# Another order in the opening of a fused attention and feed-forward kernel: mask edges, two weight loads, and layer 2 among the value products

## The chip, the cores and the metric

The kernel runs on one core of a Trainium2 chip. The metric is the device time of one execution in microseconds (us), as the median of several runs. Five engines matter: TensorE (PE in the profile; its weight loads are shown apart as PEld), VectorE (DVE), ScalarE (ACT), GpSimd (POOL) and SyncE (SP). They run independently of each other and wait for each other through semaphores. Each engine works through its own instructions in the order in which the program lists them, so an instruction that waits holds back all that stands behind it on its engine.

## The reference

First comes an attention with a window: of 576 positions in each of 8 batches and 8 heads, each attends to those at most 32 away. Its result, 4608 tokens of 512 numbers, goes through a feed-forward block of two matrix products.

```python
scores = scale * np.matmul(q, k.transpose(0, 1, 3, 2))
mask = np.abs(pos[:, None] - pos[None, :]) <= window
scores = np.where(mask, scores, -1000000000.0)
attn = np.exp(scores - max); attn = attn / (sum + 1e-09)
x = np.matmul(attn, v)            # to 4608 x 512
h = x @ w_in                      # 512 x 2048
g = h * (1.0 / (1.0 + np.exp(-1.702 * h)))
out = (g @ w_out).astype(np.float32)   # 2048 x 512
```

Inputs and output are float32 in device memory; the kernel computes in 16-bit types and sums in float32.

## The kernel before, in words

**Units and tiles.** The 4608 tokens are cut into 36 units u of 128 tokens for the attention, and into 9 tiles t of 512 tokens for the feed-forward part; tile t takes units 4t to 4t+3. For one unit the steps are: `scores(u)` (line 248), 24 small products on PE, then two exponentials on ACT, one for each half of the heads, which give `p`; `band(u)` (line 272), one multiplication on DVE of `p` by the mask; `values(u)` (line 280), 16 products on PE, listed as `pv`; `norm(u)` (line 298), a reciprocal and a multiplication on DVE that give `x`. `x_T` or `x_T2` (line 327) then transposes `x` on PE and copies it to `xT` for the first layer.

**Where the results lie.** Products land in the accumulation memory, whose banks have names: "t" (two banks), "A", "B", "C", "E" and, for layer 2, "LA" and "LB". A bank is used again only after its last reader is done: `scores(6, "t")`, `values(4, "t")`, `values(6, "t")` and `x_T2(6, "t", ...)` use "t" in turn, so each waits for the exponential, the norm or the copy that reads the one before. `values(5, "AC")` and `values(7, "AC")` do the same with "A" and "C".

**The mask.** `mask` holds four blocks of 64 columns. Ordinary units use blocks 1 and 3. A unit with a batch border takes block 0 or 2 in their place: `band` (lines 273 to 277) picks block 0 for unit 4, which is the first such unit. `setup_mask` (line 99) writes all four blocks alike; `cut_mask` (line 108), four small fills on POOL (line 111), sets the outer edges of blocks 0 and 2 to zero. Thus `band(4)` must wait for the first two of these fills.

**Values.** `values(u)` reads the rows of `v` as they are (`ve`, from `load_v`, line 194) and shifted by half a unit (`vo`). `odd_v(u)` (line 208) makes `vo` of unit u from two halves, the first of `ve[u+1]` and the second of `ve[u]`, with one copy for each; lines 218 and 220 tell them apart.

**Loads.** All loads are issued by POOL, in the order of the program: `load_kq` (line 125, staging tiles `kst` and `qst`), `load_v` (line 199), `load_v_part` (line 205), `load_w1` (line 115, w_in) and `load_w2(c)` (line 119, quarter c of w_out, 512 KB in the kernel's type). They land in the tiles `w1` and `w2`, both listed as `w`.

**Layers.** In the opening, layer 1 of tile 0 runs as plain products: `layer1_plain` (line 392), eight products of 256 columns into one bank, and a gelu on ACT (line 404). Layer 2 of tile 0 comes from `layer2_plain(0, 0)` and `layer2_plain(0, 1)` (line 478): a list `l2` of 64 single products of 512 columns, here called parts. `do(l2, n)` issues the next n of them. Part 4c' to 4c'+3 read rows 2c' and 2c'+1 of `w2`, so parts 0 to 7 of the list need quarter 0 of w_out, parts 8 to 15 quarter 1, parts 16 to 23 quarter 2 and parts 24 to 31 quarter 3. From tile 1 on both layers multiply with seven products in place of eight; `l1_group` (line 421) is one fourth of layer 1 of a tile, into which parts of layer 2, value products and, for tile 1, transposes of later `k` and `q` (`T_pe`, line 235) are woven. `x_sums` (line 363) makes the sums of `xT` that it needs, and stands between the opening and the first such group.

**The order around the change** is written out by hand in `opening` (line 576) and runs from its first loads to `do(self.l2, 4)` at line 712. After it come `x_sums(1)` and `first_layer1` (line 869), with `fetch` (line 714) issuing the loads of later units.

Of the kernel before, what the change touches and what calls it, by code (L numbers as in the profile page):

```python
# [26 lines left out]
class _Kernel:  # L27
# [548 lines left out]
    def opening(self):  # L576

        nc, dve, act, pool = self.nc, self.nc.vector, self.nc.scalar, self.nc.gpsimd
        self.setup()
        for i in range(8):  # L580
            dve.memset(self.idle[:, 64 * i:64 * i + 64], 0.0)
        dve.memset(self.spark, 0.0)
        for t in self.ve:
            dve.memset(t[:, :, self.D:], 1.0)
        self.load_first("k", 0)
        self.load_first("q", 0)
        make_identity(nc, self.ident)
        act.activation(self.spark, self.spark, AF.Exp)
        for u in (0, 1, 2):
            self.load_v(u)  # L590
        self.load_first("k", 1)
        self.load_first("q", 1)
        self.load_w1(0)
        self.setup_mask()
        self.load_v(3)
        self.load_v_part(512, 64)
        self.load_w1(1)
        self.load_w1(2)
        self.load_four("k")
        self.odd_v(3, pool)  # L600
        self.load_four("q")
        self.load_w1(3)
        self.load_v_part(576, 64)
        dve.tensor_copy(self.identh, self.ident)
        self.keep_busy(30, "E", 192)
        self.T_first("k", 0, "AC", (dve, act))
        self.keep_busy(3, "E", 512)
        self.T_first("q", 0, ("LA", "LB"), (dve, act))
        self.keep_busy(4, "E")
        self.load_v(5)  # L610
        self.load_w2(0)
        self.load_v(6)
        self.load_v(7)
        self.load_v_part(1024, 64)
        self.load_w2(1)
        self.load_v_part(1088, 64)
        for c in (2, 3):
            self.load_w2(c)
        self.load_kq("k", 8)
        self.scores(0, "t")  # L620
        self.scores(1, "AC")
        self.odd_v(0, dve)
        self.odd_v(1, dve, (1,))
        self.keep_busy(6, "E")
        self.band(0)
        self.odd_v(1, dve, (0,))
        self.band(1)
        self.values(0, "t")
        self.keep_busy(4, "E")
        self.values(1, "AC")  # L630
        self.norm(0)
        self.norm(1)
        self.T_first("k", 1, "BE", (act, act))
        self.T_first("q", 1, ("LA", "LB"), (act, dve))
        self.x_T(0, "B", dve)
        self.x_T(1, "E", dve)
        self.odd_v(2, dve, (1,))
        self.scores(2, "t")
        self.scores(3, "AC")
        gelus = []  # L640

        def l1(half, d, tag):
            self.layer1_plain(0, d, half, tag)

        l1(0, 0, "B")
        l1(0, 1, "E")
        self.band(2)
        self.odd_v(2, dve, (0,))
        self.band(3)
        self.values(2, "t")  # L650
        self.norm(2)
        self.values(3, "AC")
        self.norm(3)
        self.keep_busy(4, "LA", 512)
        l1(0, 2, "LA")
        self.x_T2(2, "A", dve)
        l1(0, 3, "LB")
        dve.tensor_copy(self.k_first, self.kT[0][:, :, 0:64])
        dve.tensor_copy(self.v_first, self.ve[0][0:64])
        for i in (3, 1, 2):  # L660
            self.w1_sums((i,), 0)
        self.cut_mask()
        for u in (6, 7):
            self.odd_v(u, pool)
        for u in (8, 9, 10, 11):
            self.fetch(u)
        l1(1, 0, "B")
        l1(1, 1, "E")
        l1(1, 2, "LA")
        l1(1, 3, "LB")  # L670
        halo = self.kT[4]
        self.T_four("k", "AC", (dve, dve))
        dve.tensor_copy(self.kT[4][:, :, 0:64], halo)
        self.w1_sums((4,), 0)
        l1(0, 4, "B")
        l1(0, 5, "E")
        self.T_four("q", "AC", (dve, act))
        l1(1, 4, "LB")
        l1(1, 5, "LA")
        for i in (3, 1):  # L680
            self.w1_sums((i,), 1)
        self.odd_v(4, dve)
        self.odd_v(5, dve, (1,))
        self.scores(4, "t")
        self.scores(5, "AC")
        for d, tag in ((6, "B"), (7, "E")):
            self.layer1_plain(0, d, 0, tag, gelus)
        self.scores(6, "t")
        self.do(self.l2, 4)
        self.scores(7, "AC")  # L690
        self.do(gelus)
        self.do(self.l2, 4)
        self.band(4)
        self.band(5)
        self.band(6)
        self.odd_v(5, dve, (0,))
        self.values(4, "t")
        self.norm(4)
        self.values(5, "AC")
        self.norm(5)  # L700
        self.band(7)
        self.values(6, "t")
        self.norm(6)
        l1(1, 6, "B")
        self.values(7, "AC")
        self.norm(7)
        l1(1, 7, "E")
        self.do(self.l2, 4)
        self.x_T2(4, "A", act)
        self.do(self.l2, 4)  # L710
        self.x_T2(6, "t", dve)
        self.do(self.l2, 4)

# [222 lines left out]
```

## Time and profile before

| quantity | value |
|---|---|
| median of 3 runs | 286.01 us (285.79 to 286.49) |
| profiled execution | 287.79 us |
| its span, first to last instruction | 286.1 us |
| mean granted TensorE clock | 0.994 |
| PE busy | 275.1 us (96%) |
| DVE busy | 215.2 us (75%) |
| ACT busy | 194.1 us (68%) |
| POOL busy | 131.3 us (46%) |

All times below are microseconds from the start of the span. A line of the timeline holds the start, the busy time, the engine, the line of the code, the operation, the tile written and the tile read, the shape, and the number of instructions that were merged. A bracket at its end gives how long the engine had been idle before, and which event seems to have ended that. Busy times of neighbouring instructions overlap, so the pace of a series is better taken from the starts. A line of the waits holds who waited for whom, the total, how often, and the longest. A line of the windows holds a stretch, its length, the busy time of each engine with its number of instructions, the granted TensorE clock, the share of the DMA engines, and the rate. A line of the DMA issues holds what is loaded, its number and size, and the time from the issue to the landing.

### The profile page before, as it was taken

To read this page: it belongs to the slowest core of one execution; us is meant where nothing else is said; L and a number is where in the kernel's file an instruction comes from. 1 tells how busy PE (TensorE), PEld (TensorE's weight loads), DVE (VectorE), ACT (ScalarE), POOL (GpSimd) and SP (SyncE) were. 2 spreads that over 40 slices of the span, in tenths; PEclk is the share of its full clock that TensorE was granted. 3 is DMA by queue.
4 is the path that set the end of the run, shared out by engine and by line. 5 is a ranking of instruction groups with operands and counts; after the bars stand their busy time and mean duration, and the time that the engine had idled before them with its cause. 6 is when DMAs were issued, how large, how long until landed. Compare 5 with 4: busy or idle time off the path is not lost.

```text
span 286.1 us, 9072 instructions
## 1 busy us (share of the span) xinstructions
PE 275.1 (96%) x3737; PEld 228.3 (80%) x3739; DVE 215.2 (75%) x502; ACT 194.1 (68%) x341; POOL 131.3 (46%) x199
## 2 busy tenths in 40 slices
PE   7889879999999999999999999999999999999994
PEld 6568746777778888888888889888888888888883
DVE  1777684898777988798879787888788888945631
ACT  2675863789787769676966896689658875567410
POOL 8965498798399828548165808340110000000000
PEclk9999998999999999999999999999999999999999
DMA  8999999999999999999999999995642030202033
GB/s 92 181 196 199 182 202 158 139 168 142 172 120 144 198 125 191 152 180 175 156 119 180 151 159 121 169 130 134 130 58 81 16 112 18 76 0 76 0 113 112
DMA packets 148026, 37.37 MB, mean 131 GB/s; under 512 B 135952, under 2 KB 143632, under 8 KB 147984
## 3 DMA queue, kind: packets, MB, share of 16 engines
q0 software_dynamic: 105504, 18.42, 89.3%
q1 hardware_dynamic: 42032, 17.84, 34.4%
q8 instruction: 29, 0.48, 0.7%
q10 hardware_dynamic: 448, 0.52, 0.6%
q14 instruction: 13, 0.11, 0.1%
HBM read 36.83 MB, written 9.44 MB: 162 GB/s over the span
## 4 chain that ended last, share of the span: by engine, by line
PE 76%; DMA 12%; POOL 6%; DVE 3%; issue 2%; ACT 0%; POOLq 0%
PE o L70 37%; PE h L70 32%; DMA w<-in_moe_w_out_dram 4%; DMA w<-in_moe_w_in_dram 4%; PE pv L70 3%; PE sc L70 3%; DMA ve<-in_v_dram 2%; DMA kst<-in_k_dram 2%; POOL ve L199 2%; POOL kq L144 1%; DVE b L360 1%; DVE h L446 1%; POOL o_sb L178 1%; PE tp L336 1%; POOL mask L105 0%
## 5 line engine op out<-in xcount | busy, mean ns | idle before, releaser
L433 ACT ACTIVATE g<-h 128x512 f16<-128x512 f32 x128 | 72.1, 598 | 35.7 <-PE h L70 34.9
L70 PEld LDWEIGHTS <-g 128*128 128x128 f16 x576 | 54.7, 98 | 10.4 <-issue 0.5
L70 PEld LDWEIGHTS <-a 128*128 128x128 f16 x512 | 49.3, 97 | 10.9 <-issue 0.7
L70 PE MATMUL h<-xs,a 128*128 128x256 f16 x384 | 57.6, 272 | 0.2
L70 PEld LDWEIGHTS <-w 128*128 128x128 f16 x512 | 49.3, 98 | 8.3 <-DMA w<-in_moe_w_in_dram 1.3
L70 PE MATMUL h<-xT,w 128*128 128x256 f16 x384 | 54.9, 277 | 0.7 <-DMA w<-in_moe_w_in_dram 0.7
L70 PE MATMUL o<-w,g 128*128 128x256 f16 (+1 forms) x320 | 55.4, 295 | 0.2 <-DMA w<-in_moe_w_out_dram 0.2
L199 POOL DMA_DIRECT2D ve<-in_v_dram x37 | 31.9, 866 | 33.5 <-issue 30.5
L70 PEld LDWEIGHTS <-gs 128*128 128x128 f16 x384 | 36.7, 98 | 4.7
L267 ACT ACTIVATE p<-sc 128x512 bf16<-128x512 f32 x72 | 36.8, 616 | 2.7 <-PE sc L70 2.6
L70 PE MATMUL o<-b,gs 128*128 128x256 f16 x256 | 37.7, 273 | 0.0
L70 PE MATMUL o<-b,g 128*128 128x256 f16 x256 | 37.3, 273 | 0.0
L446 DVE TENSOR_TENSOR h<-h,s 128x512 f32<-128x512 f32 x32 | 22.4, 699 | 17.8 <-PE h L70 17.5
L131 POOL DMA_DIRECT2D kst<-in_k_dram x31 | 26.4, 855 | 11.1 <-DMA ve<-in_v_dram 4.9
L67 ACT COPY h<-h 128x512 f32<-128x512 f32 x32 | 18.9, 589 | 16.4 <-PE h L70 15.9
L308 DVE TENSOR_TENSOR x<-pv,rec 128x256 f16<-128x256 f32 (+1 forms) x53 | 27.6, 520 | 1.8
L218 POOL COPY vo<-ve 64x264 int32<-64x264 int32 x31 | 15.7, 505 | 28.9 <-PE pv L70 24.9
L131 POOL DMA_DIRECT2D qst<-in_q_dram x35 | 28.1, 805 | 1.3 <-issue 1.2
L278 DVE TENSOR_TENSOR p<-p,mask 128x1024 bf16<-128x1024 bf16 x36 | 24.8, 697 | 4.8 <-POOL mask L111 3.4
L452 DVE TENSOR_TENSOR h<-h,s 128x512 f32<-128x512 f32 x32 | 22.4, 699 | 4.4 <-PE h L70 3.8
L67 ACT COPY s<-h 128x512 f32<-128x512 f32 x32 | 19.3, 602 | 1.1
L70 PE MATMUL h<-xs,w 128*128 128x256 f16 x128 | 19.2, 273 | 0.0
(86 smaller groups left out, 364.6 us busy)
## 6 DMA issues: line engine op xcount, KB each, us to landing
out_dram<-o_sb SPq DMA_DIRECT2D x33, 256.0 KB, 3.5
ve<-in_v_dram POOLq DMA_DIRECT2D x31, 128.0 KB, 5.5
kst<-in_k_dram POOLq DMA_DIRECT2D x25, 128.0 KB, 6.2
qst<-in_q_dram POOLq DMA_DIRECT2D x21, 128.0 KB, 5.3
w<-in_moe_w_in_dram POOLq DMA_DIRECT2D x4, 512.0 KB, 9.1
w<-in_moe_w_out_dram POOLq DMA_DIRECT2D x4, 512.0 KB, 11.8
qst<-in_q_dram POOLq DMA_DIRECT2D x7, 96.0 KB, 5.6
ve<-in_v_dram POOLq DMA_DIRECT2D x10, 64.0 KB, 7.5
```

Of the source, the lines that this page charges most:

```text
L67: (eng.copy if eng is self.nc.scalar else eng.tensor_copy)(out, in_)
L70: self.nc.tensor.matmul(out, lhsT, rhs, start=start, stop=stop, skip_group_check=True)
L131: self.nc.gpsimd.dma_start(t[off:off + n], src[b, :, s:s + n, :].rearrange("h s d -> s h d"))
L144: self.nc.gpsimd.dma_start(self.stage["first"][c, part], src[0, :, lo:lo + n, :].rearrange("h (p j) d -> p h j d", j=j))
L199: self.nc.gpsimd.dma_start(t[off:off + n, :, :self.D], self.v[b, :, s:s + n, :].rearrange("h s d -> s h d"))
L218: eng.tensor_copy(words(vo[64:128]), words(self.ve[u % 9][64:128]))
L267: self.nc.scalar.activation(p[:, eo].rearrange("k h s -> k (h s)"), sc[eo], AF.Exp, scale=self.scale)
L278: (eng or self.nc.vector).tensor_mul(pv, pv, msk.to_broadcast([128, 8, 2, SQ]))
L308: dve.tensor_mul(x[:, 4 * at:4 * (at + n), :].rearrange("p (b h) d -> p b h d", b=n), acc[:, :, :, :D], r.to_broadcast([128, n, 4, D]))
L433: act.activation(g[:, f, 256 * half:256 * half + 256], bank.rearrange("p (i n) -> p i n", i=2), AF.Gelu_apprx_sigmoid)
L446: dve.tensor_add(e, b, s7)
L452: dve.tensor_add(c, b, s7)
```

## The change

All of it lies in `opening`. The loads of quarters 2 and 3 of w_out and of `k` of unit 8 leave their place behind `load_v_part(1088, 64)` and stand behind `cut_mask`. No other load stands between the two places. At the end of the opening, two of the `odd_v`, `band`, `norm` and `values` steps change places, and the parts of layer 2 are dealt out otherwise: before 4, 4, 4 and 4 of them (ahead of `band(4)`, and three times from `l1(1, 7, "E")` on), after it 1, 3, 4, 4 and 4, of which 12 now stand among the value products and the two products of layer 1, and 4 at the end.

```diff
         self.load_v_part(1088, 64)
-        for c in (2, 3):
-            self.load_w2(c)
-        self.load_kq("k", 8)
         self.scores(0, "t")
...
         self.cut_mask()
+        for c in (2, 3):
+            self.load_w2(c)
+        self.load_kq("k", 8)
         for u in (6, 7):
             self.odd_v(u, pool)
...
         self.do(gelus)
-        self.do(self.l2, 4)
+        self.do(self.l2, 1)
         self.band(4)
         self.band(5)
+        self.odd_v(5, dve, (0,))
         self.band(6)
-        self.odd_v(5, dve, (0,))
         self.values(4, "t")
         self.norm(4)
+        self.do(self.l2, 3)
         self.values(5, "AC")
+        self.band(7)
         self.norm(5)
-        self.band(7)
         self.values(6, "t")
         self.norm(6)
-        l1(1, 6, "B")
+        self.do(self.l2, 4)
         self.values(7, "AC")
         self.norm(7)
+        l1(1, 6, "B")
+        self.do(self.l2, 4)
         l1(1, 7, "E")
-        self.do(self.l2, 4)
         self.x_T2(4, "A", act)
-        self.do(self.l2, 4)
         self.x_T2(6, "t", dve)
         self.do(self.l2, 4)
```

## The prediction

> **What bounds the kernel now.** I read the page's head first (span 286.1 us, PE busy 96%), then a table of stretches, then the list of waits, and only then the timelines of the four engines around the edit.
>
> ```profile
> 34.77:38.18 3.41, 3.17 (x72) 1.68 (x71) 1.29 (x2) 3.22 (x7) 2.27 (x7) 1.00 1.56 192
> 38.18:41.59 3.41, 1.72 (x39) 1.38 (x40) 3.31 (x10) 2.13 (x3) 3.29 (x6) 1.00 1.31 205
> 41.59:45.00 3.41, 3.35 (x30) 2.04 (x28) 2.40 (x7) 0.89 (x2) 3.16 (x4) 0.50 1.73 180
> ...
> 48.22:245.00 196.78, 196.58 (x2683) 164.32 (x2682) 165.13 (x374) 148.07 (x262) 95.75 (x142) 1.00 1.40 134
> ```
>
> From 48.22 on PE is busy 196.58 of 196.78 us: there it is the bound, and every instruction behind that point moves with it. So what the change is worth is the time at which PE reaches 48.22, the first product of `l1_group(1, 0)`. Ahead of it lie two losses. From 38.18 to 41.59 PE is busy 1.72 of 3.41 us. From 41.59 to 45.00 it is busy, but the granted clock is 0.50, so that half of 3.41, 1.70 us, is lost. Both come from one cause:
>
> ```profile
> DVE p L278 <- POOL mask L111: 3.4, 1, 3.4
> ```
>
> ```profile
> 22.18 0.79 POOL L119 DMA_DIRECT2D w<-in_moe_w_out_dram  x1
> ...
> 28.48 0.76 POOL L119 DMA_DIRECT2D w<-in_moe_w_out_dram  x1 [1.50 <-DMA o_sb<-in_q_dram]
> 30.88 0.70 POOL L205 DMA_DIRECT2D ve<-in_v_dram  x1 [1.64 <-DMA w<-in_moe_w_in_dram]
> 31.57 1.50 POOL L119 DMA_DIRECT2D w<-in_moe_w_out_dram  x2
> 35.66 0.89 POOL L131 DMA_DIRECT2D kst<-in_k_dram  x1 [2.59 <-DMA w<-in_moe_w_out_dram]
> 36.58 0.51 POOL L111 MEMSET mask<- 64x32 bf16 x4
> ...
> 39.53 0.40 POOL L220 COPY vo<-ve 64x264 int32<-64x264 int32 x1
> ```
>
> `band(4)` waits 3.4 us on DVE for the fills of the mask, and these stand on POOL behind `load_kq("k", 8)`, which waits 2.59 us for a load to land. I count the loads: that one is the 27th issued, and what lands is quarter 0 of w_out, the 19th. In the same way the 23rd (28.48) waits for the 15th and the 24th (30.88) for the 16th. So a load waits here for the landing of the one eight before.
>
> **The first edit, on POOL.** It moves three load issues behind the four fills; nothing is added. In the new order the fills follow the issue of 30.88, at about 31.6. They have nothing to wait for: `band(0)` to `band(3)` read blocks 1 and 3, and the fills write 0 and 2. The issues of 31.57 come 0.51 us later, at 32.1, and what they must wait for, the 17th and the 18th load, has landed, as they don't wait at 31.57 now. What is late next is `load_kq("k", 8)`: it still waits for quarter 0, to 35.66, and what is queued behind it is no longer the mask but `odd_v(6)` and `odd_v(7)`, 0.51 us earlier than before. So the last of these four copies ends near 39.4, where it ended at 39.93. Do the two quarters land later?
>
> ```profile
> w<-in_moe_w_out_dram POOLq DMA_DIRECT2D x1, 512.0 KB, 13.2
> ve<-in_v_dram POOLq DMA_DIRECT2D x1, 128.0 KB, 13.2
> ...
> w<-in_moe_w_out_dram POOLq DMA_DIRECT2D x1, 512.0 KB, 10.9
> ...
> w<-in_moe_w_out_dram POOLq DMA_DIRECT2D x2, 512.0 KB, 11.7
> ```
>
> In the DMA issues these rows stand for the loads issued at 22.18 and right behind it at 22.9 (quarter 0, `ve` of unit 6), at 28.48 (quarter 1) and from 31.57 on (quarters 2 and 3, median); the last number is the time to landing. Landings follow the order of issue: quarter 0 at 35.4, unit 6 at about 36.1, quarter 1 at 39.4. Quarters 2 and 3, issued 0.75 apart, land at 43.6 in the mean; POOL meets the later of them at 45.2 (a row below), so quarter 2 is there at about 42.4. An issue that then waits some 10 us behind older bytes loses nothing by coming 0.5 us later: I take zero. The other end is 0.5 us, without that cover, and as PE wants quarter 2 at 44.14 (below), it would cost nothing either. Below zero it can't come, as the order of the loads is unchanged.
>
> **The second edit, on DVE.** What is left for `band(4)` is its exponentials.
>
> ```profile
> 33.62 3.04 ACT L267 ACTIVATE p<-sc 128x512 bf16<-128x512 f32 x6
> 36.84 1.08 ACT L267 ACTIVATE p<-sc 128x512 bf16<-128x512 f32 x2 [0.18 <-PE sc L70]
> ...
> 44.71 0.60 ACT L404 ACTIVATE g<-h 128x512 f16<-128x512 f32 x1 [1.93 <-PE h L70]
> 46.24 1.01 ACT L67 COPY xT<-tp 128x1024 f16<-128x1024 f16 x1 [0.94 <-PE tp L336]
> ```
>
> ```profile
> 36.89 2.31 DVE L278 TENSOR_TENSOR p<-p,mask 128x1024 bf16<-128x1024 bf16 x3 [3.38 <-POOL mask L111]
> 39.12 0.49 DVE L220 COPY vo<-ve 64x264 int32<-64x264 int32 x1
> 39.54 0.18 DVE L307 RECIPROCAL rec<-pv 128x8 f32<-128x8 f32 x1
> ...
> 40.37 0.17 DVE L307 RECIPROCAL rec<-pv 128x4 f32<-128x4 f32 x1
> ...
> 41.47 0.68 DVE L278 TENSOR_TENSOR p<-p,mask 128x1024 bf16<-128x1024 bf16 x1
> ```
>
> Six exponentials take 3.04 us, so pairs are done at about 34.7, 35.7 and 36.66, and the fourth pair at 37.92. With a band at 0.68: `band(4)` 34.75 to 35.45, `band(5)` 35.7 to 36.4, the `vo` copy of unit 5 (0.4 to 0.49, its source landed at 36.1) to 36.8, `band(6)` to 37.5. A norm from "t" takes 0.83 (39.54 to 40.37), one from "A" and "C" 1.10 (40.37 to 41.47). `norm(4)` waits for `values(4)`, about 37.55, and ends at 38.4; `band(7)` ends at 39.05, `norm(5)` at 40.15, `norm(6)` at 41.0, `norm(7)` at 42.1. All instructions are the old ones; DVE gains 2.1 us at its first band, and it is PE that then sets the pace.
>
> **The third edit, on PE.** The walk starts at 36.74, behind `scores(7)`, which nothing of the change reaches.
>
> ```profile
> 36.74 1.04 PE L70 MATMUL o<-w,g 128*128 128x512 f16 x4
> ...
> 38.45 0.22 PE L70 MATMUL pv<-ve,p 128*64 128x65 bf16 x1 [0.29 <-DVE p L278]
> 39.67 0.19 PE L70 MATMUL pv<-vo,p 128*64 128x65 bf16 x1 [1.01 <-DVE vo L220]
> ...
> 40.51 0.22 PE L70 MATMUL pv<-ve,p 128*64 128x65 bf16 x1 [0.42 <-DVE x L308]
> ...
> 40.89 1.26 PE L70 MATMUL h<-xT,w 128*128 128x256 f16 x8
> ...
> 44.47 1.29 PE L70 MATMUL o<-w,g 128*128 128x512 f16 x4
> ...
> 46.91 0.61 PE L336 MATMUL tp<-identh,x 128*128 128x128 f16 x8
> 47.35 1.03 PE L70 MATMUL o<-w,g 128*128 128x512 f16 x4
> 48.22 0.60 PE L70 MATMUL h<-xT,w 128*128 128x256 f16 x4
> 48.65 0.38 PE L70 MATMUL o<-w,g 128*128 128x512 f16 x1
> ```
>
> Prices from starts at the full clock: four parts of layer 2 take 0.87 (47.35 to 48.22), one `values` 0.38 (40.51 to 40.89), eight products of layer 1 twice 0.43 or 0.87 (48.22 to 48.65), an `x_T2` 0.44 (46.91 to 47.35). From 36.74 to 48.22 both kernels do the same: 16 parts, 3.48; four `values`, 1.52; two layer-1 blocks, 1.74; two `x_T2`, 0.88. That is 7.62, so PE could be done at 44.36. The kernel before takes 11.48, 3.86 more: 1.72 for the three bracketed gaps, 1.70 for the clock, the rest small.
>
> The new order, step by step: one part to 36.96; `values(4)` to 37.34 (bank "t" free since 36.66); three parts to 37.99; `values(5)` to 38.37 (its last exponential was read out at 37.92, so bank "C" is free); `values(6)` must wait for `norm(4)`, 38.4, and starts at about 38.5, **0.13 waited**; it ends at 38.88. The next four parts need quarter 1, which lands at 39.4: **0.52 waited**, to 40.27. `values(7)` (`norm(5)` done at 40.15, the mask and `vo` long) to 40.65; layer 1 to 41.52; four parts to 42.39; layer 1 to 43.26; the two `x_T2` to 44.14; four parts, with quarter 2 there since 42.4 or 42.9, to 45.01. The group needs ACT's copy of the first `x_T2`: the gelu starts 0.24 behind the layer-1 block (44.71 against the 44.47 of the next row on PE) and takes 0.60, so 43.5 to 44.1, and the copy at 1.01 ends near 45.1, **0.07 waited**. PE stands at about 45.08 in place of 48.22: **3.14 us earlier**. Here the change also gives up a cover, since four parts no longer stand between the two `x_T2`; bare, it is this 0.07, at most the 0.87 of the parts.
>
> The clock is part of this sum. The stretch ahead of the slow one had PE idle for 1.69 of 3.41 us; the next idlest quoted, 34.77 to 38.18, was busy 3.17 and was not followed by a lower clock. In the new order the 3.41 us from 38.18 hold about 0.65 of waiting, 81% busy, much nearer to the second. So I take no slow stretch. [...]
>
> **What comes behind.** Quarter 3 is first used soon after the group's start, and POOL meets its landing:
>
> ```profile
> 41.23 0.89 POOL L131 DMA_DIRECT2D kst<-in_k_dram  x1
> ...
> 45.20 0.88 POOL L199 DMA_DIRECT2D ve<-in_v_dram  x1 [0.45 <-DMA w<-in_moe_w_out_dram]
> ```
>
> ```profile
> 50.44 0.81 PE L70 MATMUL o<-w,g 128*128 128x512 f16 x3
> ...
> 54.80 0.39 PE L242 MATMUL tp<-ident,kst 128*128 128x128 bf16 x4
> ```
>
> ```profile
> kst<-in_k_dram POOLq DMA_DIRECT2D x2, 128.0 KB, 6.2
> ```
>
> It is there by 45.2; PE used it in the third part of the 50.44 row, so about 50.9, and will want it at 47.8. The next hand-over is `k` of unit 9, issued at 41.23; it lands 6.2 later, at 47.4, and is transposed on PE at 54.80, in future 51.7. With 2.6 and 4.3 us left, and 0.20 us of idling of PE in the 196.78 behind 48.22, I count the whole gain to the end.
>
> **The sum.** Against the profiled execution's span: 286.1 − 3.1 = 283.0 us; it took 287.79 as a whole, so 284.65. The median of the runs, 286.01, is 1.8 below that; I take the same difference from it: 286.01 − 3.14 = **282.9 us**.
>
> **The rivals.** (1) *The half-clock stretch stays*, because its cause is not the gaps, or because the 0.65 us fall badly with others into one stretch. Against it: the slow stretch begins exactly behind the idlest one. It gives back 1.70: 284.6 us. [...] (2) *It doesn't do what it says*: the wait on the mask is inferred, and something else held `band(4)` until 36.89. Then the bands start as before, and only `vo` ahead of `band(6)` and the parts between the values remain: `values(5)` at 38.8, `values(6)` at 40.3 behind `norm(4)`, `values(7)` at 42.1 behind `norm(5)`, the group at about 46.5, a gain of 1.7 with the full clock and none with the slow stretch: 284.3 to 286.0 us. Against it: 36.89 lies just behind the second fill. (3) *Slower*: the part that now comes early meets quarter 1 late. PE would stand in front of it from 38.88. If quarter 1 takes the 13.2 us of quarter 0 and not 10.9, it lands at 41.7, 2.3 us later, and a stretch with that much idling brings back the half clock, 1.70: −3.14 + 2.3 + 1.7, so 286.9 us. It decides from a landing at about 40.9 on: 1.5 of further waiting and 1.7 for the clock equal the gain. Against it: no load ahead of quarter 1 is touched.
>
> **How the numbers follow.** Forecast 0.78, rival 1 0.13, rival 2 0.05, rival 3 0.04. A measurement of this kernel tells about 0.3%, 0.86 us, from no change. Forecast and rival 1 are faster, rival 2 mostly (0.03): faster 0.94, within 0.3% 0.02, slower 0.04. The range starts where all three waits vanish, 286.01 − 3.86 = 282.15, so 282.2, and goes up to rival 1 with the 0.2 us by which the runs lie below their median, 284.8.
>
> **What would show it.** The fills on POOL at about 31.6 and `band(4)` at about 34.75 show the first edit right. `values(5)` without a wait for `vo`, `values(6)` at about 38.5 and a wait for w_out of about 0.5 ahead of the parts behind it show the walk. No stretch at clock 0.50 after 41 shows the clock term. The group's first product at about 45.1, and the same work behind it in the same time, show that the gain holds. I am wrong if PE waits for a load behind 45, or for quarter 1 much longer than 0.5.

## The result, and the profile after

| | before | changed kernel |
|---|---|---|
| median of 20 runs | 286.40 us (285.59 to 287.85) | 285.37 us (284.53 to 287.10) |
| profiled execution, span | 287.79 us, 286.1 us | 284.63 us, 282.9 us |
| granted clock in it | 0.994 | 1.000 |

The ratio is 0.9967, with a 95% interval from 0.9951 to 0.9983: faster, by about 1.0 us, and outside the range of the forecast (282.2 to 284.8). Yet the profiled execution of the changed kernel has the very span that was forecast, 283.0, to 0.1 us. In that there is luck, as it is the second shortest of the 20 and 0.74 below their median. The walk through the opening came true, and the step from one execution to the median did not.

The timelines of POOL, DVE and PE of the changed kernel, in this order:

```profile
31.65 0.51 POOL L111 MEMSET mask<- 64x32 bf16 x4
32.10 1.50 POOL L119 DMA_DIRECT2D w<-in_moe_w_out_dram  x2
35.40 0.89 POOL L131 DMA_DIRECT2D kst<-in_k_dram  x1 [1.80 <-DMA w<-in_moe_w_out_dram]
...
44.79 0.88 POOL L199 DMA_DIRECT2D ve<-in_v_dram  x1 [0.57 <-DMA w<-in_moe_w_out_dram]
```

```profile
35.07 0.69 DVE L278 TENSOR_TENSOR p<-p,mask 128x1024 bf16<-128x1024 bf16 x1 [1.35 <-ACT p L267]
35.98 0.69 DVE L278 TENSOR_TENSOR p<-p,mask 128x1024 bf16<-128x1024 bf16 x1 [0.22 <-ACT p L267]
36.59 0.50 DVE L220 COPY vo<-ve 64x264 int32<-64x264 int32 x1
```

```profile
36.74 0.39 PE L70 MATMUL o<-w,g 128*128 128x512 f16 x1
37.44 0.82 PE L70 MATMUL o<-w,g 128*128 128x512 f16 x3
39.14 1.02 PE L70 MATMUL o<-w,g 128*128 128x512 f16 x4
40.53 1.05 PE L70 MATMUL h<-xT,w 128*128 128x256 f16 x8
...
44.91 0.60 PE L70 MATMUL h<-xT,w 128*128 128x256 f16 x4
```

The fills stand ahead of the loads, and `band(4)` waits no longer for the mask but for ACT, to 35.07. PE runs from 36.74 to the first `l1_group` at 44.91 with no bracket of a wait; it was forecast for 45.08. Three stretches of the windows:

```profile
38.18:41.59 3.41, 3.29 (x62) 2.34 (x62) 3.27 (x11) 2.12 (x3) 3.35 (x6) 1.00 1.31 204
41.59:45.00 3.41, 3.41 (x33) 2.45 (x32) 1.26 (x5) 2.10 (x3) 2.83 (x4) 1.00 1.76 181
...
44.91:241.69 196.78, 196.58 (x2681) 164.13 (x2680) 164.91 (x374) 147.94 (x262) 98.77 (x145) 1.00 1.52 136
```

PE is busy 3.29 of the 3.41 us in which it was idle for half before, the clock stays at 1.00, and behind 44.91 the same 196.78 us hold the same 196.58 us of work. This one execution keeps all of its gain. Why the median doesn't is a question of the spans and clocks of single executions.

### The profile page after: what moved, and what is told of

Its sections match the earlier page's. It is cut to its first block, busy times and chain, and to the rows that moved or that the text cites. A ratio compares the mean times of both kernels' runs of the same rounds, so it can differ in the third digit from the quotient of the medians.

```text
span 282.9 us, 9074 instructions
## 1 busy us (share of the span) xinstructions
PE 274.9 (97%) x3739; PEld 228.3 (81%) x3739; DVE 214.9 (76%) x502; ACT 193.9 (69%) x341; POOL 132.2 (47%) x199
## 4 chain that ended last, share of the span: by engine, by line
PE 81%; DMA 9%; POOL 4%; DVE 3%; issue 1%; ACT 1%; POOLq 0%
PE o L70 39%; PE h L70 34%; DMA w<-in_moe_w_out_dram 4%; PE pv L70 4%; PE sc L70 3%; DMA o_sb<-in_q_dram 3%; DMA ve<-in_v_dram 2%; POOL kq L144 1%; DVE b L360 1%; POOL ve L199 1%; PE tp L336 1%; DVE h L446 1%; ACT g L433 1%; DVE o_sb L67 0%; POOL mask L105 0%
## 5 line engine op out<-in xcount | busy, mean ns | idle before, releaser
L70 PE MATMUL h<-xT,w 128*128 128x256 f16 x384 | 53.9, 273 | 0.3 <-DMA w<-in_moe_w_in_dram 0.2
L218 POOL COPY vo<-ve 64x264 int32<-64x264 int32 x31 | 14.5, 468 | 27.6 <-PE pv L70 23.5
```

The costliest lines, as they stand in the source:

```text
L70: self.nc.tensor.matmul(out, lhsT, rhs, start=start, stop=stop, skip_group_check=True)
L218: eng.tensor_copy(words(vo[64:128]), words(self.ve[u % 9][64:128]))
```

## The experiments

Two theories stood first. **C:** the half-clock stretch that the profile before shows, 1.70 us, belongs to some executions only; a usual one gains only what the waits cost, 1.4 us. **D:** it is in every execution before, and the changed kernel loses elsewhere. Later a second pair was needed for the changed kernel's own losses: **Q**, it meets quarter 1 of w_out too early; **L**, the loss lies behind the opening, where PE catches up with transfers; and **E**, neither.

### Each half alone, the gaps filled, and the changed kernel again

`e1_mask_early` is the first edit alone, `e2_order_only` the second and third. `e3_gap_filled` is the kernel before with:

```diff
+        acc = self.acc[4][0]
         self.norm(4)
+        self.fill_gap(acc, 11)     # 11 products of zeros, 240 columns, into columns 264 to 503 of the bank
         self.values(5, "AC")
...
+        self.fill_gap(acc, 3)      # the same, 3 times, into the bank of values(5)
         self.values(6, "t")
```

> Only the two quarters of w_out and k of unit 8 are moved behind the mask fills; bands, values, norms and parts of layer 2 stand as before. Theory C: the half-clock stretch of 1.70 us that the profile before shows belongs to a part of the executions only, so the change is worth its waits alone, about 1.4 us in a usual run. Walked like the forecast, this half brings the first l1_group to about 45.6, where the whole change has 45.1: the usual run is 0.9 us faster than before. Theory D: the half-clock stretch is in every execution before, and the changed kernel loses time elsewhere in its usual runs: this half is then 2.6 us faster than before minus whatever is lost, with a loss to be seen behind 45.

> Only the other half: loads and mask fills as before, bands, vo copy, norms, values and parts in the new order. The first band starts at 36.9 as before. C: the first l1_group at about 46.5 at full clock, which is where the kernel before would be without its half-clock stretch: no difference in a usual run (within 0.4 us). D: up to 1.7 us faster, as the gaps in one stretch become shorter and the clock may stay up.

> The kernel before with 14 additional products of zeros on PE (240 columns, 0.10 us each) into unused columns of the banks, 11 ahead of values(5) and 3 ahead of values(6): they fill the waits of PE there and change nothing else. The profile shows no granted clock of 0.50 behind 41. C: the median stays within 0.4 us of before, and only the upper runs come down. D: every execution gains, about 1.7 us.

> The changed kernel again, unchanged. C: about 1.0 to 1.4 us faster than before in the median; its own profile, whatever execution it falls on, reaches the first l1_group near 45, and executions differ by what lies ahead of 31 or behind 45. D: the profile shows PE waiting or a lower clock behind 45.

| kernel | median | lowest to highest | ratio to before, 95% |
|---|---|---|---|
| before | 286.05 | 285.32 to 288.12 (32 runs) | |
| e1_mask_early | 285.60 | 285.20 to 288.06 (12) | 0.9988 (0.9966 to 1.0010) |
| e2_order_only | 286.03 | 285.54 to 287.03 (12) | 0.9991 (0.9971 to 1.0010) |
| e3_gap_filled | 288.05 | 287.91 to 290.56 (9) | 1.0081 (1.0050 to 1.0113) |
| e4_after_again | 285.60 | 284.30 to 287.35 (12) | 0.9977 (0.9951 to 1.0004) |

The list of clocks answers C against D. For 121 executions of the kernel before, beside the 20 of the result and the first profile, the mean granted clock is on record. In 18 of them it is 0.994, as in the first profile, and their median is 287.62 us; in the 103 others it is 0.997 or more, and their median is 286.00. Half the clock lost for 3.41 of 286 us makes a mean of 0.994, and the difference of the medians, 1.62, is near the 1.70 of the first profile. Only the first profile shows the stretch itself, so that the 18 hold it is read from their clock; with that, 1.62 us is its price, paid in about one execution of seven. **C holds**: the forecast took its 1.70 us from a median that didn't contain them. None of 59 executions of the changed kernel shows that clock.

The timelines of PE tell the halves apart; the first two rows are of `e1_mask_early`, the others of `e2_order_only`:

```profile
38.97 0.22 PE L70 MATMUL pv<-ve,p 128*64 128x65 bf16 x1 [0.65 <-DVE x L308]
...
45.41 0.60 PE L70 MATMUL h<-xT,w 128*128 128x256 f16 x4
```

```profile
39.67 0.22 PE L70 MATMUL pv<-ve,p 128*64 128x65 bf16 x1 [1.02 <-DVE x L308]
...
45.99 0.60 PE L70 MATMUL h<-xT,w 128*128 128x256 f16 x4
```

With the mask early alone, `values(6)` still waits 0.65 for `norm(4)` and the group starts at 45.41; with the order alone the bands start late, the wait is 1.02 and the group starts at 45.99 (46.5 was expected). Each half gives a part, in the order of the walk. In time, neither half can be told from no change, nor can the whole change in this group of runs, where its median, 285.60, is that of `e1_mask_early`.

`e3_gap_filled` failed as an experiment on the clock: a median within 0.4 us of before, or 1.7 below it, was expected, and it came out 2.0 above. The additional products go into columns that nobody reads, but the program makes them wait for `norm(4)` reading other columns of the bank:

```profile
40.12 1.29 PE L70 MATMUL pv<-idle 128*128 128x240 bf16 x11 [2.25 <-DVE x L308]
...
42.40 0.47 PE L70 MATMUL pv<-idle 128*128 128x240 bf16 x3 [0.61 <-DVE x L308]
```

```profile
37.40:40.80 3.40, 1.15 (x24) 1.07 (x24) 2.64 (x5) 2.61 (x4) 3.23 (x6) 1.00 1.37 201
40.80:44.20 3.40, 2.79 (x51) 2.04 (x51) 2.39 (x7) 0.00 (x0) 3.40 (x5) 1.00 1.50 189
```

Instead of filling gaps it made one of 2.25 us. Behind a stretch with PE busy for only 1.15 of 3.40 us the clock stayed at 1.00 in this trace; in another of the nine executions its mean is 0.991, which fits a slow stretch there.

Does idling then not matter? In the first profile the record of the clock starts 4.04 us into the span, and the clock changes 37.55, 40.96 and 283.31 us behind that; in the first profile of the changed kernel it starts at 6.18 and changes 276.48 us behind that. These are 11, 12, 83 and 81 times 3.41 us. In the 3.41 us ahead of a drop to half clock PE was busy for 1.72 us in the first profile (38.18 to 41.59) and for 0.00 in the changed kernel (279.25 to 282.66, behind PE's end; the clock is 0.51 from there to the end of the span). The stretch of 1.15 us was cut by hand. Cut at 39.14, its gap falls into two:

```profile
35.73:39.14 3.41, 2.15 (x46) 1.07 (x45) 2.63 (x4) 3.38 (x6) 3.05 (x8) 1.00 1.40 199
39.14:42.56 3.42, 1.83 (x29) 1.55 (x29) 1.69 (x7) 0.90 (x2) 3.42 (x5) 1.00 1.28 205
```

PE is busy 2.15 and 1.83 us in them, so how idle a stretch comes out depends on where it is cut. What brings the drop was not shown: only one stands in the middle of a program, and behind 3.41 us with PE busy for 1.57, at PE's end in the first profile (280.51 to 283.93), the clock stayed at 1.00.

### Single executions

> The kernel before again, one look. C: most likely an execution without the half-clock stretch, span near 284.2 us, with the same waits of PE between 37 and 41 and the first l1_group at about 46.5. D: the half clock from about 41 to 45 again, span near 286.

> The changed kernel, one look, to see what its executions differ by (spans 282.6 to 285.7 at the same mean clock). Theory Q: quarter 1 of w_out is now read within 0.5 us of its landing, so a late landing delays PE directly; a longer execution shows PE waiting for w_out ahead of the parts behind values(6). Rival L: the lost time lies behind 45, where PE catches up with the loads of k, q and v.

> The same look at the changed kernel again. Q: in a longer execution PE waits for quarter 1 of w_out near 39. L: it waits behind 45.

> A third look at the changed kernel. Q: in a longer execution PE waits for quarter 1 of w_out near 39. L: it waits behind 45.

The kernel before, in `f1_before_look`, took 285.44 us, span 283.7. Its first band, its group, and its windows:

```profile
35.84 2.31 DVE L278 TENSOR_TENSOR p<-p,mask 128x1024 bf16<-128x1024 bf16 x3 [2.40 <-POOL mask L111]
```

```profile
45.90 0.60 PE L70 MATMUL h<-xT,w 128*128 128x256 f16 x4
```

```profile
38.18:41.59 3.41, 2.45 (x63) 1.81 (x58) 3.27 (x10) 2.77 (x4) 3.35 (x6) 1.00 1.32 203
41.59:45.00 3.41, 3.41 (x34) 2.37 (x33) 1.38 (x5) 1.68 (x3) 2.30 (x4) 1.00 1.77 182
```

The wait for the mask is there, 2.40 us in place of 3.38, and the clock stays up. The group starts at 45.90, not at 48.22: 1.70 of the 2.32 us is the clock, and most of the rest is that the mask came a microsecond sooner in this execution (the first band starts at 35.84 and not at 36.89), by inference because quarter 0 of w_out, for which POOL waited 2.59 us ahead of the fills in the first profile, landed sooner. The three executions of the changed kernel took 284.48, 284.80 and 284.56 us, with the group at 44.79, 45.15 and 44.73. So at full clock the change is worth about 1.1 us at the group. In the first and the third PE stands in front of quarter 1, as Q has it:

```profile
39.08 1.02 PE L70 MATMUL o<-w,g 128*128 128x512 f16 x4 [0.32 <-DMA w<-in_moe_w_out_dram]
```

```profile
39.02 1.02 PE L70 MATMUL o<-w,g 128*128 128x512 f16 x4 [0.43 <-DMA w<-in_moe_w_out_dram]
```

But all three are among the shorter executions and say nothing of the longer ones.

### Quarter 1 taken out of the way

`g1_no_quarter1` and `g2_only_quarter0` change line 487, so that PE does the same work on rows that are there early (the output is then another), and `g3_quarter1_halved` changes the load:

```diff
-            self.mm(st[i], self.g[t][:, f, lo:lo + 128], self.w2[:, f, :], start=(f == 0))
+            self.mm(st[i], self.g[t][:, f, lo:lo + 128], self.w2[:, f - 4 if 4 <= f < 8 else f, :], start=(f == 0))
```

```diff
-            self.mm(st[i], self.g[t][:, f, lo:lo + 128], self.w2[:, f, :], start=(f == 0))
+            self.mm(st[i], self.g[t][:, f, lo:lo + 128], self.w2[:, f % 4, :], start=(f == 0))
```

```diff
-        self.load_w2(1)
+        self.load_w2_half(1, 0)    # rows 4 and 5 of w2
+        self.load_w2_half(1, 1)    # rows 6 and 7
```

> The changed kernel, but in layer 2 of tile 0 the rows of quarter 1 of w_out are replaced by those of quarter 0 (a changed computation), so PE does the same work and never waits for quarter 1 in the opening. Q: the wait of 0.2 to 0.4 us that the looks show near 39 vanishes, and the spans of repeated executions draw together at about 282.5 (median 1 us below the changed kernel's repeated runs, which lie at 283.5 to 283.9). L: spans spread from 282.5 to 285.5 as in the changed kernel, median at most 0.3 us lower.

> As the one before, but all of layer 2 of tile 0 reads rows of quarter 0 alone (a changed computation): no part waits for quarters 1, 2 or 3. Q for quarter 1 alone: the same as with quarter 1 replaced. If quarters 2 or 3 are what comes late in the longer executions, this one draws together and the other doesn't. L: neither does.

> The changed kernel with quarter 1 of w_out loaded as two loads of half the size, so that its first half, which the early parts need, can land up to 1.3 us sooner; it costs one load issue more on POOL (0.75 us) ahead of the mask, and as a load waits for the eighth before it, quarter 3 is issued only when quarter 0 has landed. Q: the wait near 39 vanishes, 0.3 us faster than the changed kernel in one look, and more in repeated runs. L: same as the changed kernel.

> The changed kernel once more, on the same chip as the three others, for comparison. Q and L: median 0.5 to 1.0 us below the kernel before, spans from 282.6 to 285.7.

Medians: before 286.16 (35 runs); without quarter 1, 285.19 (ratio 0.9961, 0.9945 to 0.9977); with quarter 0 only, 285.71 (0.9986, 0.9962 to 1.0009); halved, 285.55 (0.9971, 0.9950 to 0.9992); the changed kernel, 285.04 (0.9962, 0.9942 to 0.9983). Taking the wait for quarter 1 away didn't shorten anything. **Q falls** as the cause: the wait is real, 0.17 to 0.43 us in four traces of the changed kernel, and small. The trace of `g1_no_quarter1` shows where time goes instead, in the timelines of SyncE and PE and in the DMA issues:

```profile
96.26 3.16 SPq L233 DMA_TRANSPOSE kT<-kst  x1
```

```profile
kT<-kst SPq DMA_TRANSPOSE x1, 9.7
```

```profile
105.12 0.48 PE L70 MATMUL sc<-qT,kT 64*64 64x64 bf16 x26
105.97 0.44 PE L70 MATMUL sc<-qT,kT 64*64 64x64 bf16 x22 [0.38 <-DMA kT<-kst]
```

PE stops behind the 26th of the 48 products of `scores(18)` and `scores(19)`. The 27th is the first that reads `k` of unit 20, whose transpose by DMA was issued at 96.26 and landed 9.7 us later, at 105.96. The room that this transpose has in each trace, from its landing to the 27th product (the start of the 48 and 0.34):

| trace | room, us | trace | room, us |
|---|---|---|---|
| before, first profile | 2.00 | f3_after_look | 1.34 |
| f1_before_look | 1.84 | f4_after_look | 0.74 |
| e2_order_only | 1.74 | g4_after_again | 1.71 |
| e1_mask_early | 1.21 | h4_after_again | 0.20 |
| changed kernel, profile | 0.95 | g1_no_quarter1 | waits 0.38 |
| e4_after_again | 0.56 | g2_only_quarter0 | waits 0.20 |
| f2_after_look | 1.00 | | |

The room is 0.20 to 1.71 us in the seven traces of the changed kernel, against 1.84 and 2.00 before: what PE gained in the opening, this transpose gained only in part. A wait for it shows only in two variants.

### More room for that transpose, and none needed

`h1_turn18_early` (changed kernel) and `h2_before_turn18_early` (kernel before) move two transposes in `back`; `h3_no_k20` lets `scores(19)` do without the third.

```diff
-            self.turn(u + n + 4)
+            if (t, n) != (2, 2):
+                self.turn(u + n + 4)
+            if (t, n) == (2, 1):
+                self.turn(u + 6)
```

```diff
-        nxt = ... else self.kT[u + 1][:, :, 0:64]
+        nxt = ... else self.kT[u if u == 19 else u + 1][:, :, 0:64]
```

> The changed kernel with one step moved: the transposes by DMA of q of unit 18 and k of unit 19 are issued on SyncE one quarter of a tile earlier, ahead of two transposes of x and a store that stand in their way, so those of q 19 and k 20 behind them come some 2 us earlier too. Theory L: what the changed kernel loses in part of its executions is the wait of scores(19) for the transposed k of unit 20 near 105, which has 0.4 to 1.7 us of room in the looks and less than none in two of them: this one then draws together near 282.8 in span and is 0.4 us or more faster than the changed kernel in the median. Theory E: the losses come from somewhere else, or the DMA engines are the limit: no difference, or slower as the transposes of x come later.

> The same move in the kernel before, as a control. L: no difference from the kernel before in the usual runs (within 0.2 us), since k of unit 20 has 1.8 to 1.9 us of room there. E: faster or slower by as much as in the changed kernel.

> The changed kernel, but scores(19) takes its last 64 columns of k from unit 19 and not from unit 20 (a changed computation), so it never waits for that transpose. L: the long executions disappear or become rarer, median 0.3 us or more below the changed kernel. E: the same spread and median as the changed kernel.

> The changed kernel on the same chip as the three others, for comparison. L: its profile has little room between the landing of k of unit 20 and scores(19), and where there is none, PE waits there. E: no such wait even in a long execution.

Medians: before 285.94 (35 runs); h1, 286.44 (284.41 to 290.00; ratio 0.9994, 0.9961 to 1.0027); h2, 285.94 (1.0002, 0.9985 to 1.0018); h3, 285.14 (0.9965, 0.9944 to 0.9985); h4, the changed kernel, 285.12 (0.9970, 0.9951 to 0.9989). The control did as L said. The two others did not: without the wait for unit 20 the time is the same, and with the transposes moved up it is longer, by 1.3 us in the median. **L in its narrow form, this one transpose, falls.** In the trace of `h3_no_k20`, another transpose takes its place; DVE, then PE:

```profile
136.55 0.43 DVE L368 TENSOR_TENSOR xs<-xT 128x512 f16<-128x512 f16 x1 [1.35 <-DMA xT<-x]
```

```profile
137.04 0.61 PE L70 MATMUL h<-xs,a 128*128 128x256 f16 x4 [0.50 <-DVE xs L368]
```

Here it is a transpose of `x`, one tile later. The unaltered changed kernel meets it too. The same place in `g4_after_again`, DVE and PE, and then PE in `f1_before_look`:

```profile
135.72 0.42 DVE L368 TENSOR_TENSOR xs<-xT 128x512 f16<-128x512 f16 x1 [0.75 <-DMA xT<-x]
```

```profile
135.27 0.60 PE L70 MATMUL h<-xT,w 128*128 128x256 f16 x4
...
137.33 0.79 PE L70 MATMUL h<-xs,a 128*128 128x256 f16 x4
137.96 0.60 PE L70 MATMUL h<-xT,w 128*128 128x256 f16 x4
```

```profile
136.15 0.60 PE L70 MATMUL h<-xT,w 128*128 128x256 f16 x4
...
137.90 0.60 PE L70 MATMUL h<-xs,a 128*128 128x256 f16 x4
138.34 0.60 PE L70 MATMUL h<-xT,w 128*128 128x256 f16 x4
```

From one `h<-xT,w` row to the next PE takes 2.69 us here and 2.19 before: 0.50 us lost, in pieces too short for a bracket. DVE waits for this landing in four of the seven traces of the changed kernel (0.20 to 0.75 us), and in none of the seven of the kernel before, its two variants, the two halves and `e3_gap_filled`.

In `h1_turn18_early` the two transposes of `x` of tile 3 stand behind the ones moved up:

```profile
86.42 1.80 SPq L233 DMA_TRANSPOSE qT<-qst  x1
88.32 1.24 SPq L233 DMA_TRANSPOSE kT<-kst  x1
89.65 3.26 SPq L320 DMA_TRANSPOSE xT<-x  x2
```

They are issued at 89.65, against 86.5 to 87.8 in the traces of the changed kernel. Whether this makes its longest runs is open, as none of them was traced: four took 288.4 to 290.0 us, and three of these have a mean clock of 0.992 or 0.993, which fits a slow stretch in them.

### The whole queue relieved

`i1_after_few_stores` (changed kernel) and `i2_before_few_stores` (kernel before) leave the output of tiles 1 to 3 unwritten:

```diff
     def store(self, t, pr, o):
+        if t in (1, 2, 3):
+            return
```

> The changed kernel without the stores of the output of tiles 1, 2 and 3 (12 stores of 256 KB on SyncE left out), so that the transposes by DMA behind them on the same queue, and the DMA engines from about 89 to 175, have less to do; PE, DVE, ACT and POOL keep their work. Theory L in its wider form: the changed kernel loses again because PE, now earlier, meets transposes by DMA that do not come earlier by as much (k of unit 20 near 106, x of tile 4 near 136): the median comes down by 0.3 us or more against the changed kernel (285.1 on most chips) and the runs above 285.8 go. Theory E: the losses have nothing to do with these transposes: same median and spread as the changed kernel.

> The same left out in the kernel before, as a control. L: within 0.2 us of the kernel before in the median, as the transposes have 2 us of room there. E: as much faster as the changed kernel gets from it, or no difference in both.

Measured: `i1` 283.72 us (283.50 to 284.10, 6 runs; ratio to before 0.9916, 0.9890 to 0.9942), `i2` 285.14 (284.77 to 285.74, 12 runs; 0.9957, 0.9939 to 0.9976), before 286.06 (17 runs). The changed kernel's spread, 1.2 us in `h4_after_again` on the same chip and 2.3 to 3.1 elsewhere, is 0.6 in these 6 runs, as L says. But the control moved too, by 0.9 us where at most 0.2 was expected, or by 0.66 against the 12 of the 17 runs before at the higher clock (285.80). Span and last row of PE, first of `i1`, then of `i2`, then of `f1_before_look` and of the changed kernel's first profile:

```profile
span 281.8 us, 9048 instructions
```

```profile
276.63 1.91 PE L70 MATMUL o<-w,gs 128*128 128x256 f16 x16
```

```profile
span 283.1 us, 9048 instructions
```

```profile
277.89 1.91 PE L70 MATMUL o<-w,gs 128*128 128x256 f16 x16
```

```profile
span 283.7 us, 9072 instructions
```

```profile
277.86 1.91 PE L70 MATMUL o<-w,gs 128*128 128x256 f16 x16
```

```profile
span 282.9 us, 9074 instructions
```

```profile
277.00 1.91 PE L70 MATMUL o<-w,gs 128*128 128x256 f16 x16
```

PE ends at 278.54 and 279.80, so 3.26 and 3.30 us ahead of the end of the span. In the full kernels that distance is 3.93 (`f1_before_look`) and 3.99 (changed kernel). So 0.6 to 0.7 us of what both gain lies behind PE's end, and for the control this is all of it. Ahead of it, from the start of the group (45.93 in `i2`) to PE's end, `i2` takes 233.87 us and `f1_before_look` the same 233.87: relieving the queue gives the kernel before nothing there. The changed kernel takes 233.97 to 234.6 in its traces, `i1` 233.78, and its trace shows no wait of DVE for `xT` there. And with the queue relieved in both, the change is worth 285.14 − 283.72 = **1.42 us**. That the forecast without its clock term comes to 1.44 is luck in part: in these two traces the group starts only 1.17 us earlier.

That is L in its wider form: with the stores in place, 0.84 us are left in the median (286.00 over the 103 executions of the kernel before at the higher clock, 285.16 over 59 of the changed kernel), and the rest, 0.2 to 0.6 us by estimate, is given back to transfers that don't come earlier. Shown in traces is 0.1 to 0.7 us behind the group, most of it at the products on `x` of tile 4 in the worst of them; 14 of the 59 executions of the changed kernel took more than 286 us, and none of these was traced. Whether it is the order on SyncE or the load of the DMA engines can't be told, as both were relieved at once. No version with the whole output written was faster than the changed kernel.

## Why the prediction was wrong

**The fills and the landings: right.** Forecast at 31.6, found at 31.65; quarter 3 still met by POOL at 44.79, so the loads lost nothing by coming later.

**The walk on DVE and PE: right.** Group at 45.08 by forecast, at 44.91 in the profile and 44.6 to 45.2 in the seven traces of the changed kernel. `values(5)` doesn't wait for `vo`; the wait for quarter 1 was put at 0.52 and came to 0.17 to 0.43, in four of seven.

**The step that failed is the clock term in the sum.** The forecast said "So I take no slow stretch", which is right for the changed kernel, and then "The median of the runs, 286.01, is 1.8 below that; I take the same difference from it". That treats the difference as a constant of profiling. It isn't: time and span differ by 1.7 in both profiled executions (287.79 and 286.1, 284.63 and 282.9), so the profiled execution before was itself 1.8 us longer than a usual one, and 1.70 of that was the very stretch whose removal the forecast then counted. By the clocks, the stretch is in 18 of 121 executions. Removed from the sum, 3.14 becomes 1.44.

**The remaining wait was over-sized by about 0.3.** In the profiled execution the mask came late: the first band starts at 36.89, and in `f1_before_look` at 35.84. At full clock the group of the kernel before starts at 45.90 to 46.23 in three traces (`f1`, and `h2` and `i2`, which are changed only behind it), not at the 46.5 that the profile without its stretch implies; against 44.9 this is about 1.1.

**"I count the whole gain to the end" failed in part.** The forecast looked at the first hand-overs behind the opening, which do have room, and took from the 0.20 us of idling that nothing else was near. A wait that isn't there shows no room: `k` of unit 20 had 2.00 us in a kernel that was to move by 3.14, and the transpose of `x` of tile 4, for which nothing waits before, is met in the changed kernel. By the medians 0.2 to 0.6 us go to such transfers. Of the 3.14 us, then, 1.70 go with the clock term, about 0.3 with the wait and 0.2 to 0.6 behind the opening, and 0.5 to 0.9 are left; the medians give 0.84 at the higher clock, and 1.03 over the 20 runs of each, of which five before, from 287.40 on, probably hold the slow stretch.

**The rivals.** The first had the right price, 1.70, on the wrong kernel: the stretch does not stay, it usually isn't there. What brings it was not shown: PE is busy for 1.72 of the 3.41 us ahead of it in the first profile, and in `e3_gap_filled` the clock stayed at 1.00 behind a stretch with 1.15 of 3.40. The second rival falls with the first band, which follows ACT. The third is there in small: PE waits for quarter 1, but never for 2.3 us in a trace, and no half clock follows.

## What to carry to other kernels

Before a loss is counted as a gain, ask whether the usual run has it: a profiled execution whose time lies above the median has lost something there, and the table of stretches with the granted clock says what (here 287.79 us against 286.01, and 3.41 us at a clock of 0.50). A time saved early in an engine that is busy to the end can be given back at a later transfer that has no room (here 0.84 us were left in the medians, and 1.42 with 12 stores left out of both kernels); measure that room from landing to first use for each transfer down the program, not from the idle time of the engine. To find out whether a lost gain is in a queue, relieve the queue in both kernels, and compare the difference between the two.

## What the runs showed of the hardware that was not expected

A mean clock of 0.994, which fits a half-clock stretch, comes in 18 of 121 executions of the kernel before, and costs 1.6 us in the medians (287.62 against 286.00). In the first profile of each kernel the granted clock changes 11, 12 and 83, and 81 times 3.41 us behind the start of its record, and PE was busy for 1.72 of the 3.41 us ahead of the one drop in the middle of a program; why there is open. Leaving out 12 stores in the middle of the program brought the end of the span 0.6 to 0.7 us closer to PE's last product (3.93 and 3.99 to 3.30 and 3.26), though the last stores are the same; why is open. Transposes by DMA issued between 90 and 97 took 8.5 to 10.0 us to land in the traces of the changed kernel, against medians of 4.4 and 4.7 between 50 and 70 in its first profile; why they are slower there was not tried.
